# Sorting the first item's values from the loaded layout with strided weight loads, ahead of the key sorts

## Chip, cores, metric

One core of one Trainium2 chip. The metric is the device time of one execution in microseconds (us), read on the chip; lower is better. One execution in each job is also profiled, and all the profile lines below come from such traces.

## The reference, cut to what matters

For each of 4 items and 8 heads, a sort network is normalised to an 8 x 8 matrix P (five rounds of exp and of row and column sums). P mixes the 8 blocks (96 tokens each) of keys and of values; attention runs within a block; a two-layer network with a maximum follows over all 3072 tokens.

```python
for _ in range(5):                       # "the normalising chain"
    P = np.exp(P - max); P /= rowsum; P /= colsum
k_sorted = einsum('bhij,bhjcd->bhicd', P, k_b)     # "key sort"
v_sorted = einsum('bhij,bhjcd->bhicd', P, v_b)     # "value sort": c = 96 tokens, d = 64 columns
attn = softmax(scale * q_b @ k_sorted.T);  x = attn @ v_sorted
out = np.maximum(x @ w1, x @ w2) @ w_out
```

## The kernel before

TensorE multiplies a *stationary* operand, brought in by a weight load (LDWEIGHTS, PEld in the profile), with a *moving* one. A value sort takes v with (head, block) on 64 partitions as stationary operand, 96 tokens of one d at a time, padded to 128 columns; the moving operand is a 64 x 64 block-diagonal matrix of P. Four sorts of 16 matmuls make one item. v arrives as `(c d)` along a partition, so the 96 tokens of one d lie 64 elements apart. The kernel turns it first, with copies, to `(d c)`:

```python
    def turn_v(rows, eng, c0, c1):          # copies on ScalarE ("A") or VectorE ("D")
        dst = v_dc[rows, 0 : D * BLK].rearrange("p (d c) -> p d c", c=BLK)[:, :, c0:c1]
        src = v_raw[rows].rearrange("p (c d) -> p d c", d=D)[:, :, c0:c1]
    ...
    def sort_v(b, t, n=0, eng=None):
        ps = ps_f32("v_ps")                 # PSUM: four buffers in a ring for everything
        keep_streaming(ps, n)               # "fillers": matmuls of zeros, n columns, that keep TensorE busy
        for m in range(16):
            d = t * 16 + m
            nc.tensor.matmul(ps[:, m * 64 : (m + 1) * 64],
                v_dc[r0 : r0 + 64, d * BLK : d * BLK + 128],   # 128 neighbouring columns
                bd_v[b][r0 : r0 + 64, :], start=True, stop=True)
        evac(v_sb[...], ps[...], eng=eng)   # copy out of PSUM on ScalarE or VectorE
    ...                                     # start of the program
    keep_streaming(ps_f32("fill_ps"), 18 * 512)
    for it in range(5):
        sinkhorn(it)                        # from it = 3 on with 6 fillers of 512 columns each
        ...                                 # masks; turn_v in pieces on ScalarE at it = 2, 3
    ...
    sort_k(0, 0, 2048, "A"); sort_k(0, 1, 512, "A"); sort_k(0, 2, 256, "D")
    q_transposes(0, 0, "D")                 # needs q from HBM
    sort_v(0, 0, 256, "A"); ...; sort_v(0, 3, 384, "A")
    q_transposes(0, 1, "D"); scores(0, 0, 256); scores(0, 1, 256); values(0, 0, 512)
```

The softmax here doesn't subtract the row's maximum and nothing guards it: scores larger than these inputs give would overflow.

## Time and profile before

| | before |
|---|---|
| median (range) | 181.52 us (181.5 to 182.01), 3 runs |
| span of the profiled run, granted TensorE clock | 179.5 us, 0.999 |
| TensorE busy | 95% |
| first product of the dense layer (h_ps) starts | 25.93 us |
| TensorE's waits from 16 to 90 us | 0.22, 0.20, 0.35 and 0.60 us |

TensorE is the bound from about 16 us on. "Clock" is the granted clock as a share of full speed.

### The profile page before, as it was taken

How to read it: one execution, taken by the hardware profiler on the slowest of the kernel's cores; microseconds unless marked ns; L12 is line 12 of the kernel's file. 1: busy time of each engine (PE TensorE's matmuls, PEld its weight loads, DVE VectorE, ACT ScalarE, POOL GpSimd, SP SyncE). 2: the span in 40 equal slices, each digit the busy share in tenths (PEclk: the TensorE clock that was granted, in tenths of full speed). 3: DMA queues.
4: the chain of work that ended last, by engine and by line, in shares of the span. 5: the costliest groups of instructions: out<-in, count | busy, mean ns of one | idle time of the engine just before them, and what ended most of it. 6: DMA issues, size and time to landing. Idle time of an engine off the chain costs nothing.

```text
span 179.5 us, 4648 instructions
## 1 busy us (share of the span) xinstructions
PE 170.0 (95%) x2083; PEld 100.7 (56%) x2083; DVE 94.0 (52%) x192; ACT 91.8 (51%) x110; POOL 22.9 (13%) x39
## 2 busy tenths in 40 slices
PE   7797989999999989999989999999999999999993
PEld 2246666666565535577655554657555546554453
DVE  5878498559864395253586436156245415340210
ACT  3695876777664445368784341465833233520021
POOL 7861443200180000001000000000000000000000
PEclk9999999999999999999999999999999999999999
DMA  3999999999299991235600113200001132000333
GB/s 58 201 204 206 200 207 214 194 202 208 55 120 221 206 250 48 99 117 74 108 4 0 57 63 117 104 17 5 0 4 42 74 117 116 4 0 4 117 117 117
DMA packets 13939, 19.17 MB, mean 107 GB/s; under 512 B 800, under 2 KB 8864, under 8 KB 13920
## 3 DMA queue, kind: packets, MB, share of 16 engines
q0 software_dynamic: 10304, 12.58, 41.6%
q1 hardware_dynamic: 3328, 6.10, 8.9%
q8 instruction: 16, 0.26, 0.6%
q10 hardware_dynamic: 288, 0.20, 0.3%
q14 instruction: 3, 0.02, 0.0%
HBM read 25.17 MB, written 6.29 MB: 175 GB/s over the span
## 4 chain that ended last, share of the span: by engine, by line
PE 58%; DMA 29%; DVE 5%; issue 4%; POOL 2%; ACT 1%; POOLq 0%; DVEq 0%
PE out_ps L590 32%; PE h_ps L563 16%; DMA v_raw<-in_v_dram 10%; DMA w_sb<-in_moe_w_dram 10%; DMA q_raw<-in_q_dram 9%; PE o_ps L463 3%; PE tx_ps L495 2%; PE k_ps L371 2%; PE s_ps L438 2%; DVE g L579 2%; PE tq_ps L341 1%; DVE x L480 1%; DVE xT L105 1%; POOL v_raw L153 1%; DVE v_dc L209 1%
## 5 line engine op out<-in xcount | busy, mean ns | idle before, releaser
L590 PE MATMUL out_ps<-wo_sb,g 128*128 128x512 bf16 (+2 forms) x208 | 48.1, 363 | 0.2 <-DVE g L579 0.2
L563 PE MATMUL h_ps<-xT,w_sb 128*128 128x384 bf16 x256 | 46.1, 326 | 0.5 <-DVE g L579 0.2
L563 PEld LDWEIGHTS <-w_sb 128*128 128x128 bf16 x256 | 23.6, 97 | 15.1 <-issue 0.7
L577 ACT ACTIVATE g<-h_ps 128x768 bf16<-128x768 f32 x24 | 19.4, 811 | 23.4 <-PE h_ps L563 23.4
L446 ACT ACTIVATE e<-s_ps 96x768 bf16<-96x768 f32 x32 | 24.1, 804 | 14.0 <-PE s_ps L438 13.9
L590 PEld LDWEIGHTS <-g 128*128 128x128 bf16 x208 | 17.7, 97 | 15.8 <-issue 0.2
L590 PE MATMUL out_ps<-wc,xT 128*128 128x512 bf16 (+2 forms) x104 | 25.0, 362 | 0.0
L103 ACT COPY o<-out_ps 128x1024 f32<-128x1024 f32 x8 | 8.1, 1012 | 31.0 <-PE out_ps L590 27.3
L480 DVE TENSOR_TENSOR x<-o_ps,rs 96x512 bf16<-96x512 f32 x32 | 22.0, 687 | 1.1
L474 DVE RECIPROCAL rs<-o_ps 96x8 f32<-96x8 f32 x32 | 6.4, 201 | 27.4 <-PE o_ps L463 27.2
L590 PEld LDWEIGHTS <-xT 128*128 128x128 bf16 x104 | 9.9, 98 | 10.9
L209 DVE COPY v_dc<-v_raw 64x1536 bf16<-64x1536 bf16 (+2 forms) x9 | 14.1, 1583 | 1.8 <-DMA v_raw<-in_v_dram 1.7
L463 PEld LDWEIGHTS <-e 96*128 96x128 bf16 x256 | 11.2, 98 | 6.5 <-DVE x L480 1.1
L579 DVE TENSOR_SCALAR g<-h_ps 128x768 bf16<-128x768 f32 x8 | 7.7, 958 | 13.5 <-PE h_ps L563 10.6
L463 PE MATMUL o_ps<-v_sb,e 96*128 96x65 bf16 x256 | 12.9, 193 | 1.3 <-DVE x L480 0.6
L105 DVE CAST v_sb<-v_ps 96x1024 bf16<-96x1024 f32 x7 | 8.5, 1217 | 5.9 <-PE v_ps L392 3.9
L103 ACT CAST v_sb<-v_ps 96x1024 bf16<-96x1024 f32 x9 | 8.7, 1010 | 3.4 <-PE v_ps L392 2.6
L103 ACT CAST kT<-k_ps 128x1024 bf16<-128x1024 f32 x10 | 9.5, 1024 | 0.0
L103 ACT COPY xT<-tx_ps 128x768 bf16<-128x768 bf16 x11 | 8.8, 797 | 1.5 <-PE tx_ps L495 1.5
L438 PEld LDWEIGHTS <-kT 64*128 64x128 bf16 x256 | 6.2, 94 | 5.4 <-issue 4.4
L129 POOL DMA_DIRECT2D q_raw<-in_q_dram x4 | 3.6, 901 | 43.0 <-DVE q_pair L326 40.7
L438 PE MATMUL s_ps<-qT,kT 64*128 64x96 bf16 x256 | 9.0, 204 | 0.1
(78 smaller groups left out, 162.5 us busy)
## 6 DMA issues: line engine op xcount, KB each, us to landing
out_dram<-o SPq DMA_DIRECT2D x11, 512.0 KB, 2.8
k_raw<-in_k_dram POOLq DMA_DIRECT2D x12, 256.0 KB, 13.7
q_raw<-in_q_dram POOLq DMA_DIRECT2D x4, 768.0 KB, 8.9
v_raw<-in_v_dram POOLq DMA_DIRECT2D x6, 384.0 KB, 12.0
w_sb<-in_moe_w_dram POOLq DMA_DIRECT2D x3, 512.0 KB, 15.7
wo_sb<-in_moe_w_out_dram POOLq DMA_DIRECT2D x2, 512.0 KB, 19.9
v_raw<-in_v_dram POOLq DMA_DIRECT2D x3, 256.0 KB, 5.1
w_sb<-in_moe_w_dram POOLq DMA_DIRECT2D x2, 256.0 KB, 14.3
```

What stands on the lines that cost most here:

```text
L103: nc.scalar.copy(out=out_ap, in_=in_ap)
L105: nc.vector.tensor_copy(out=out_ap, in_=in_ap)
L209: nc.vector.tensor_copy(out=dst, in_=src)
L438: nc.tensor.matmul(ps[:, h2 * 512 + ii * BLK : h2 * 512 + (ii + 1) * BLK], kT[b][rows, (hp * 8 + i) * BLK : (hp * 8 + i) * BLK + 128], rhs ...
L446: nc.scalar.activation(out=e[:, 0 : 8 * BLK].rearrange("p (t f) -> p t f", t=2), in_=ps[0:BLK].rearrange("p (t f) -> p t f", t=2)[:, :, 0 ...
L463: nc.tensor.matmul(ps[:, h2 * 512 + ii * 65 : h2 * 512 + (ii + 1) * 65], e[:, (h2 * 4 + ii) * BLK : (h2 * 4 + ii) * BLK + 128], v_sb[:, m0 ...
L474: nc.vector.reciprocal(out=rs, in_=ov[:, :, :, 64])
L480: nc.vector.tensor_tensor(out=x, in0=ov[:, :, :, 0:D], in1=rs.to_broadcast([BLK, 2, 4, D]), op=ALU.mult,)
L563: nc.tensor.matmul(h_ps[t][:, m * 512 : m * 512 + TCH], w1_sb[:, hp, fb * 128 : (fb + 1) * 128], xT[:, b % 2, ch, hp % 2, hp // 2, :], sta ...
L577: nc.scalar.activation(out=g, in_=src, func=AF.Relu)
L579: nc.vector.tensor_scalar(out=g, in0=src, scalar1=0.0, scalar2=None, op0=ALU.max)
L590: nc.tensor.matmul(dst, g_tiles[b, ch, m // 2][:, m % 2, off : off + 128] if m < NFB else xT[:, b % 2, ch, hp % 2, hp // 2, off : off + 12 ...
```

## The change

The intent: drop the turn of item 0's v (five copies) and load the weights with a step of 64 elements straight from the loaded layout, so that the value sorts no longer hang on the turn. They can then run ahead of the key sorts, in the time in which TensorE waited for q. Fillers are shortened.

```diff
-    v_raw = big.tile([128, BLK * D], BF16, tag="v_raw", name="v_raw")
+    v_raw = big.tile([128, 128 * D], BF16, tag="v_raw", name="v_raw")
+    nc.vector.memset(v_raw[:, BLK * D :], 0.0)
...
-        kinds = [1] if b % 2 else [1, 0]
+        kinds = [1] if b % 2 else [0, 1]     # the matrix for the values is built first
...
-                v_dc[r0 : r0 + 64, d * BLK : d * BLK + 128],
+                v_raw[0:64].rearrange("p (c d) -> p d c", d=D)[:, d]
+                if b == 0
+                else v_dc[r0 : r0 + 64, d * BLK : d * BLK + 128],
...
-    turn_v(first, "A", ...)                  # all five turns of item 0
-    sort_k(0, 0, 2048, "A")
-    sort_k(0, 1, 512, "A")
-    sort_k(0, 2, 256, "D")
+    sort_v(0, 0, 2048, "A")
+    sort_v(0, 1, 128, "D")
+    sort_k(0, 0, 128, "A")
+    sort_k(0, 1, 128, "D")
+    sort_k(0, 2, 128, "A")
     q_transposes(0, 0, "D")
-    sort_v(0, 0, 256, "A")
-    sort_v(0, 1, 384, "A")
-    sort_v(0, 2, 384, "D")
-    sort_v(0, 3, 384, "A")
+    sort_v(0, 2, 128, "A")
+    scores(0, 0, 256)
+    sort_v(0, 3, 128, "D")
+    scores(0, 1, 256)
     q_transposes(0, 1, "D")
-    scores(0, 0, 256)
-    scores(0, 1, 256)
-    values(0, 0, 512)
+    values(0, 0, 256)
```

More of the change, by code (lines that the diff above doesn't have):

```diff
@@ L204, in turn_v @@
         dst = v_dc[rows, 0 : D * BLK].rearrange("p (d c) -> p d c", c=BLK)[:, :, c0:c1]
-        src = v_raw[rows].rearrange("p (c d) -> p d c", d=D)[:, :, c0:c1]
+        src = v_raw[rows, 0 : BLK * D].rearrange("p (c d) -> p d c", d=D)[:, :, c0:c1]
         if eng == "A":
@@ L647 @@
             selections(0)
-            turn_v(first, "A", 0, 11)
-        if it == 3:
-            turn_v(first, "A", 11, 22)
-    turn_v(first, "A", 22, 40)
     block_diagonals(0)
-    turn_v(first, "D", 56, 96)
-    turn_v(first, "A", 40, 56)
     SC, VA, TR = att(0)
-    sort_k(0, 0, 2048, "A")
-    sort_k(0, 1, 512, "A")
-    sort_k(0, 2, 256, "D")
+    sort_v(0, 0, 2048, "A")
[3 more added lines that the diff above has]
+    sort_k(0, 2, 128, "A")
     q_transposes(0, 0, "D")
-    sort_v(0, 0, 256, "A")
-    sort_v(0, 1, 384, "A")
-    sort_v(0, 2, 384, "D")
-    sort_v(0, 3, 384, "A")
+    sort_v(0, 2, 128, "A")
+    scores(0, 0, 256)
+    sort_v(0, 3, 128, "D")
+    scores(0, 1, 256)
     q_transposes(0, 1, "D")
-    scores(0, 0, 256)
-    scores(0, 1, 256)
-    values(0, 0, 512)
+    values(0, 0, 256)
     SC[2]()
```

## The prediction

> **What bounds the kernel now.** I read three views in this order: the page (busy time and the slices), TensorE's instructions in order of time for the first 45 us, and those of VectorE and ScalarE for the same stretch. The page says that TensorE is the bound:
>
> ```profile
> PE 170.0 (95%) x2083; PEld 100.7 (56%) x2083; DVE 94.0 (52%) x192; ACT 91.8 (51%) x110; POOL 22.9 (13%) x39
> PE   7797989999999989999989999999999999999993
> DMA  3999999999299991235600113200001132000333
> ```
>
> From the sixth slice (4.5 us each) on, TensorE is nearly always full; the only gap over 0.35 us after 16 us is one of 0.60 us at 64.4. So what the change can win lies in the start: whatever moves the first dense products earlier moves the end by as much, unless a load holds them. The start, as TensorE lived it (start, duration, what, and in brackets the idle time before it):
>
> ```profile
> 12.46 0.69 PE L371 MATMUL k_ps<-bd,k_raw 64*64 64x64 bf16 x32
> 15.91 0.86 PE L346 MATMUL tq_ps<-ident,q_raw 128*64 128x128 bf16 x24 [0.97 <-DMA q_raw<-in_q_dram]
> 16.92 0.64 PE L392 MATMUL v_ps<-bd,v_dc 64*128 64x64 bf16 x16
> 19.43 0.64 PE L392 MATMUL v_ps<-bd,v_dc 64*128 64x64 bf16 x16
> 20.00 0.86 PE L346 MATMUL tq_ps<-ident,q_raw 128*64 128x128 bf16 x24
> 22.26 0.42 PE L463 MATMUL o_ps<-v_sb,e 96*128 96x65 bf16 x8
> 22.61 0.51 PE L438 MATMUL s_ps<-qT,kT 64*128 64x96 bf16 x16
> 25.93 0.81 PE L563 MATMUL h_ps<-xT,w_sb 128*128 128x384 bf16 x4
> ```
>
> The reader is to see: the key sorts come first, TensorE then waits 0.97 us for the load of q, and all four value sorts run after that wait, on the path to the scores and the first product. They can't run earlier because the turned copy of v isn't complete until the last of these ends, near 15.3 us (VectorE) and 13.75 us (ScalarE):
>
> ```profile
> 12.91 2.38 DVE L209 COPY v_dc<-v_raw 64x2560 bf16<-64x2560 bf16 x1
> 9.73 4.02 ACT L207 COPY v_dc<-v_raw 64x1152 bf16<-64x1152 bf16 x2
> ```
>
> [...] these rows show the 128-column load shorter than the 64-column one.
>
> ```profile
> L392 PEld LDWEIGHTS <-v_dc 64*128 64x128 bf16 x64 | 2.1, 95 | 0.6 <-issue 0.5
> L346 PEld LDWEIGHTS <-q_raw 128*64 128x64 bf16 x48 | 1.4, 110 | 1.1 <-DMA q_raw<-in_q_dram 1.1
> ```
>
> [...] here the granted clock is 0.999 over the whole span[...].
>
> **The change, part by part.**
>
> *Removed:* five turning copies of item 0. On ScalarE they are 1.39 + 1.38 + 4.02 = about 6.8 us, on VectorE 2.38 us. All lie before 15.3 us. ScalarE's do not delay its exponentials (each starts 0.04 us after the VectorE result it needs), so the copies cost only through the order that they force: value sorts after key sorts, and evacuations queued behind copies.
>
> *Added:* one VectorE memset of 1024 words of 4 bytes. The memset of 256 words took 0.27 us, so about 1.07 us, at 1.4 to 2.5 us or a little later. The first row sum starts at 2.61, so the normalising chain slips by 0 to 0.4 us. Most of that falls into slack ahead of the load of q. I count 0.1.
>
> *Moved:* two value sorts and all key sorts now stand ahead of the q turn; value sorts 2 and 3 stand around the first scores. The order of instructions also shows a gain that the diff doesn't: the static balance of evacuations hands one relu of item 0 from VectorE to ScalarE, and reshuffles six evacuations of item 2 (four of values, one of q, several relus).
>
> *The sum.* From starts in TensorE's timeline: one value sort takes 17.49 - 16.92 = 0.57 us (36 ns a matmul), one key sort 0.63, one half of the q turn 0.79, 8 scores 0.28. A filler of 256 columns costs 0.21 from start to start, of 384 0.27, of 512 0.32; the line through these gives 0.16 for 128. If a strided load costs no more than a contiguous one, TensorE runs: value sort 0 at 12.46 (after the same 2048-column filler), to 13.03; value sort 1 to 13.76; three key sorts at 0.79 each to 16.13. q has landed at 15.9, so the 0.97 us wait is filled with work. Then q turn to 16.92, value sort 2 to 17.65. The first scores need the q evacuation on VectorE (0.96 us from 16.98), so 17.95 to 18.25; value sort 3 to 18.98; scores 1 to 19.47; second q turn to 20.26. VectorE evacuates value sort 3 (1.22 us from 19.0) and then the second q half, to about 21.3; the third and fourth scores (22.61 before) need that half. So they start at about 21.3: **1.3 us earlier.**
>
> Does a weight load eat that? The difference of the first weight tile is done on GpSimd at 22.94, and the first product, at 25.93 - 1.3 = 24.6, stays behind it. The tighter one is the third difference on VectorE, whose weights landed at 27.2 (chain of waits: the load of w from 9.78 for 17.39 us). It started at 27.31; VectorE would now reach it at 26.0 and wait 1.2 us. Behind it on VectorE stand 1.23 us (evacuation of w2T) and 0.68 us (fourth difference), so the next softmax quotient would start at 29.65 and not at 29.3, its result come at 30.5, and the third pair of h products, which takes over its PSUM buffer, could start at 30.5; the full shift asks for 31.83 - 1.3 = 30.53. It just fits. So 1.3 us passes, but a larger gain would not.
>
> Then strided loads: 4 sorts x 16 = 64 loads, all on this path now. Each extra 10 ns costs 0.64 us. At 36 ns a matmul the gain is 1.3; at 56 it is gone.
>
> Later: with one relu less on VectorE (0.96 us), the four turns of item 1 and the two q copies can begin earlier, the loads behind them are issued earlier, and the 0.60 us wait at 64.4 us (VectorE waiting for v, then TensorE for VectorE) should shrink. I count 0.3. Sum with an allowance of 8 ns a load (64 x 8 = 0.5 us): 181.52 - 1.3 - 0.3 + 0.5 + 0.1 = **180.5 us**, 0.6% less.
>
> **The rivals.**
>
> *A: strided loads are free.* [...] so does the change's own tuning (short fillers look measured). Then 179.7 to 180.1. Chance 0.45.
>
> *B: [...]* About 50 to 65 ns a matmul, 64 x 14 to 29 ns = 0.9 to 1.9 us: the gain is cancelled, 180.5 to 181.8. Chance 0.27.
>
> *C: [...] the penalty is several-fold.* [...] Against it: nobody would shift these sorts onto the path without having seen them run. Chance 0.2.
>
> *D: the weights' landing binds.* TensorE arrives earlier and waits, with the gain falling to 0.5: 181. By my sums it just doesn't. It is the wait that would take the place of the one removed: 0.03.
>
> *E: fewer fillers let the clock drop* near 16 to 24 us, costing 1 to 3 us. The gaps I foresee are under 1 us, so I give it little, 0.05.
>
> **Range and chances.** A and B together fill 179.5 to 181.8; half of C reaches to 184. Range 179.3 to 184.0. Faster by over 2% needs under 177.9, a gain of 3.6 us. That is more than all the value sorts' share of the start, and the weights' landing at 27.2 stands against it: 0.03. Slower by over 2% needs over 185.2, so loads at least (185.2 - 180.0)/64 = about 80 ns dearer than contiguous ones: 0.11. The rest, 0.86, is within 2%.
>
> **What would show each step right or wrong.** Right: no turning copies before 16 us; value sort 0 at about 12.5 us, of 0.6 us; no wait for q over 0.3 us; the scores that stood at 22.61 at about 21.3, the first h products at 24.6; VectorE waiting near 26 to 27.2 for weights. A value sort's start to next start of 0.57 says A, 0.8 to 1.0 says B, 1.7 or more says C. D shows as an idle TensorE at 28 to 31 us, E as a clock under 0.99 in the slices. The prediction is wrong if loads of value sorts are over 100 ns apart, [...] or if the reshuffled evacuations of item 2 add waits at 85 to 95 us where VectorE held TensorE for only 0.24 us twice.

## The result, and the profile after

| | before | after |
|---|---|---|
| median (range) | 181.74 us (181.5 to 182.01), 4 runs | 186.69 us (185.72 to 187.79), 4 runs |
| ratio of fast runs | | 1.0277, 95% interval 1.0227 to 1.0326 |
| span, clock of the profiled run | 179.5 us, 0.999 | 185.7 us, 0.963 |
| first h product starts | 25.93 us | 32.00 us |

Ratios here are the mean time of one kernel's fast runs over that of the other's in the same rounds, so not quite the ratio of the medians quoted. All eight runs count as fast (within 1.5% of the fastest of the same kernel). The change makes the kernel 2.8% slower; the range of the prediction ended at 184.0.

The page of the changed kernel; the rows are 40 slices of 4.6 us, in tenths:

```profile
PE 178.3 (96%) x2083; PEld 108.4 (58%) x2083; DVE 92.4 (50%) x191; ACT 85.3 (46%) x107; POOL 23.0 (12%) x39
...
PE   7899999989999999999999999999999999999993
...
PEclk9997855999999999999999999999999999999999
```

TensorE is busier than before and the time is longer: busy time alone cannot tell useful work from slow work. The last row shows what no row before showed: a clock below full speed in four slices. TensorE's order of time (start, duration, what):

```profile
12.70 1.60 PE L393 MATMUL v_ps<-bd,v_raw 64*128 64x64 bf16 x16
14.40 1.60 PE L393 MATMUL v_ps<-bd,v_raw 64*128 64x64 bf16 x16
16.09 0.94 PE L372 MATMUL k_ps<-bd,k_raw 64*64 64x64 bf16 x32
...
19.39 1.01 PE L347 MATMUL tq_ps<-ident,q_raw 128*64 128x128 bf16 x24
...
20.49 1.64 PE L393 MATMUL v_ps<-bd,v_raw 64*128 64x64 bf16 x16
...
22.71 1.63 PE L393 MATMUL v_ps<-bd,v_raw 64*128 64x64 bf16 x16
...
25.03 1.49 PE L347 MATMUL tq_ps<-ident,q_raw 128*64 128x128 bf16 x24
...
27.57 0.83 PE L441 MATMUL s_ps<-qT,kT 64*128 64x96 bf16 x16 [0.29 <-DVE qT L105]
...
32.00 1.49 PE L566 MATMUL h_ps<-xT,w_sb 128*128 128x384 bf16 x4
```

A value sort takes 14.23 - 12.70 = 1.53 us from its start to the next start, where it took 0.57. Over its 16 matmuls that is 96 ns each, where it was 36, start-up included. (From matmul to matmul inside a contiguous sort it is 29 ns, inside a strided one about 90.) The wait for q is gone, as meant: the q turn starts at 19.39 with no idle time before it. But it starts 3.5 us later than before. Then ordinary work is slow too: the second q turn takes 1.49 us, the first 1.01, and both took 0.86 before; four h products take 1.49 us in place of 0.81. The table of stretches says why (columns: stretch and its length; busy time of each engine with its instructions; the clock; DMA share; GB/s):

```profile
core 0: us, PE busy (x) PEld busy (x) DVE busy (x) ACT busy (x) POOL busy (x), PEclk, DMA share, GB/s
14.00:16.00 2.00, 2.00 (x22) 1.85 (x21) 0.00 (x0) 1.01 (x1) 0.00 (x0) 1.00 1.26 203
16.00:18.00 2.00, 2.00 (x65) 1.75 (x66) 1.22 (x1) 0.93 (x1) 0.54 (x1) 0.58 1.28 202
...
20.00:22.00 2.00, 2.00 (x33) 1.84 (x27) 0.96 (x1) 0.51 (x1) 2.00 (x2) 1.00 1.27 201
...
24.00:26.00 2.00, 2.00 (x33) 1.57 (x34) 1.22 (x1) 0.81 (x1) 0.53 (x1) 0.50 1.27 213
26.00:28.00 2.00, 1.71 (x31) 1.41 (x29) 1.40 (x3) 0.00 (x0) 0.41 (x1) 0.50 1.22 200
```

At 14 to 16 us, with a full clock, the strided loads are already slow; the loads are therefore not slow because of the clock. By the clock records of the trace it falls twice: at 16.32 us (back at 19.74), just after the first two strided sorts, and at 23.15 (back at 33.39), within the fourth. From the first h product to the end the two kernels take the same time: 185.7 - 32.0 = 153.7 us against 179.5 - 25.9 = 153.6. So the net loss lies in the start. (The two totals hide a small exchange: the changed kernel runs the first 1.4 us of that part at half clock, about 0.7 us lost by estimate, and saves about as much later, as e10 will show.)

### The profile page after: what moved, and what is told of

Read it like the earlier page. It is cut to its first block, busy times and chain, and to the rows that moved or that the text cites. A ratio compares the mean times of both kernels' runs of the same rounds, so it can differ in the third digit from the quotient of the medians.

```text
span 185.7 us, 4642 instructions
## 1 busy us (share of the span) xinstructions
PE 178.3 (96%) x2083; PEld 108.4 (58%) x2083; DVE 92.4 (50%) x191; ACT 85.3 (46%) x107; POOL 23.0 (12%) x39
## 4 chain that ended last, share of the span: by engine, by line
PE 73%; DVE 12%; DMA 7%; ACT 3%; issue 1%; POOL 1%; DVEq 0%; ACTq 0%
PE out_ps L593 31%; PE h_ps L566 21%; DMA v_raw<-in_v_dram 6%; PE o_ps L466 3%; PE v_ps L393 3%; PE k_ps L372 3%; DVE v_dc L210 3%; PE tx_ps L498 3%; PE s_ps L441 3%; ACT g L580 3%; DVE x L483 2%; PE tq_ps L342 1%; PE tq_ps L347 1%; DVE xT L105 1%; PE tw_ps L521 1%
## 5 line engine op out<-in xcount | busy, mean ns | idle before, releaser
L566 PE MATMUL h_ps<-xT,w_sb 128*128 128x384 bf16 x256 | 46.8, 329 | 0.4 <-ACT g L580 0.2
L580 ACT ACTIVATE g<-h_ps 128x768 bf16<-128x768 f32 x28 | 22.6, 812 | 24.8 <-PE h_ps L566 24.8
L105 DVE CAST v_sb<-v_ps 96x1024 bf16<-96x1024 f32 x9 | 10.9, 1219 | 12.1 <-PE v_ps L393 9.0
L466 PEld LDWEIGHTS <-e 96*128 96x128 bf16 x256 | 12.1, 102 | 5.9 <-DVE x L483 0.6
L466 PE MATMUL o_ps<-v_sb,e 96*128 96x65 bf16 x256 | 13.8, 200 | 0.7 <-ACT e L449 0.4
L210 DVE COPY v_dc<-v_raw 64x1536 bf16<-64x1536 bf16 (+1 forms) x8 | 11.8, 1489 | 1.3 <-DMA v_raw<-in_v_dram 1.2
L105 DVE COPY qT<-tq_ps 128x1536 bf16<-128x1536 bf16 x8 | 7.5, 953 | 5.6 <-PE tq_ps L342 3.7
L441 PEld LDWEIGHTS <-kT 64*128 64x128 bf16 x256 | 6.7, 98 | 5.9 <-issue 4.6
L441 PE MATMUL s_ps<-qT,kT 64*128 64x96 bf16 x256 | 9.6, 213 | 0.4 <-DVE qT L105 0.3
L103 ACT CAST v_sb<-v_ps 96x1024 bf16<-96x1024 f32 x7 | 6.9, 1009 | 5.9 <-PE v_ps L393 5.9
```

The source lines that it names most:

```text
L103: nc.scalar.copy(out=out_ap, in_=in_ap)
L105: nc.vector.tensor_copy(out=out_ap, in_=in_ap)
L210: nc.vector.tensor_copy(out=dst, in_=src)
L441: nc.tensor.matmul(ps[:, h2 * 512 + ii * BLK : h2 * 512 + (ii + 1) * BLK], kT[b][rows, (hp * 8 + i) * BLK : (hp * 8 + i) * BLK + 128], rhs ...
L466: nc.tensor.matmul(ps[:, h2 * 512 + ii * 65 : h2 * 512 + (ii + 1) * 65], e[:, (h2 * 4 + ii) * BLK : (h2 * 4 + ii) * BLK + 128], v_sb[:, m0 ...
L566: nc.tensor.matmul(h_ps[t][:, m * 512 : m * 512 + TCH], w1_sb[:, hp, fb * 128 : (fb + 1) * 128], xT[:, b % 2, ch, hp % 2, hp // 2, :], sta ...
```

## Experiments

Theory: (1) a load of 128 columns 64 elements apart costs some 60 ns more than one of neighbours, 64 times 60 = 3.8 us; (2) in a strided sort TensorE streams 64 columns in 96 ns and waits for weights for most of it, and this low share of streaming lets the clock fall; (3) the new order by itself gains. Rivals: the shortened fillers let the clock fall; or the new order itself loses.

To compare runs I use a measure worked out from the traces, the *streaming share*: moving columns of all matmuls that start within a stretch of 3.4 us, divided by 2.4 columns a ns and the length of the stretch (a share can come out over 1, because starts are counted). The rate is that of the traces, rounded up: six products of 512 columns take 1.30 us at full clock, 2.36 columns a ns. The 3.4 us are the shortest stretch at half clock: between 10 and 70 us each such stretch in these traces lasts 3.41 us or two, three or four times that (3.41 and 10.24 in the changed kernel, 6.83 in e1, 13.65 in e2). That the clock follows the share over just this length is my assumption.

### e1_contig: the change with contiguous loads (wrong result)

```diff
-                v_raw[0:64].rearrange("p (c d) -> p d c", d=D)[:, d]
+                v_raw[0:64, d * BLK : d * BLK + 128]
```

> The changed kernel with one thing undone: the value sorts of item 0 load 128 neighbouring columns of the raw v in place of columns 64 elements apart (so the result is wrong, on purpose). Same order, fillers, memset, waits. My theory (the strided loads cost 96 ns a matmul in place of 36, and their low share of streaming lets TensorE's clock drop): value sort 0.57 us, clock 0.99 or more, 180.2 us, 1 to 1.6 us under the kernel before. Rival F (the shortened fillers let the clock drop, not the loads): clock stays near 0.965 and the time is 182.5 to 184. Rival G (the new order itself loses): slower than before with a full clock.

Measured: 181.74 us (180.57 to 182.79), ratio 1.0013 (0.9967 to 1.0059). The value sort is back at 0.57 us. But the gain of the order isn't there, and the clock of the four runs was 0.981, 1.0, 1.0 and 0.991. Loads explain most of the 5 us, but both my theory (180.2, full clock) and the rivals miss. The trace shows something that nobody had named:

```profile
18.70 0.29 PE L393 MATMUL v_ps<-bd,v_raw 64*128 64x64 bf16 x4
20.20 0.52 PE L393 MATMUL v_ps<-bd,v_raw 64*128 64x64 bf16 x12 [1.21 <-issue]
```

TensorE stops for 1.2 us in the middle of a value sort, between two matmuls that need nothing from anybody ("issue": no releaser in the profile). e6 and e10 take this up.

### e2_wide: the change with a wider moving operand

```diff
-                ps[:, m * 64 : (m + 1) * 64],
+                ps[:, m * 64 : m * 64 + wide],     # wide = min(192, what is left of the 512 columns)
...
-                bd_v[b][r0 : r0 + 64, :],
+                bd_wide...[0:64, 0:wide]           # bd_v, then 128 columns of zeros
```

> The changed kernel with the strided loads kept, but each matmul of item 0's value sorts streams up to 192 columns in place of 64 (the rest are zeros, overwritten by the next matmul; the result stays right). [...] My theory: sort stays at 1.53 to 1.6 us, clock goes back to 0.99 or more, about 184.0 us: the clock's share, 2.5 to 3 us, is won back, the loads' share of 3.8 us isn't. If the clock does not hang on the share of streaming: no change from 186.7.

Measured: 185.14 us (183.93 to 188.51), correct; ratio of the three fast runs 1.0174. By execution: 183.93 and 184.11 us with a clock of 1.0, 185.14 with 0.991, 187.03 with 0.972, 188.51 with 0.962. The sort stays at 1.58 us, where 64 columns took 1.53 to 1.57, so the extra columns are nearly free under the loads (192 columns are 81 ns by estimate, at the measured 2.36 a ns, and a strided sort takes 96 ns a matmul). With a full clock the time is the 184.0 that I expected. But the clock was full in only two of five executions. The traced one (0.962) again has a stall with no releaser, 0.39 us at 22.46, and the clock falls just there. e13 finishes this.

### e3_old_order: the kernel before with strided loads only

```diff
 (kernel before; turns, order and fillers kept, memset of the tail added)
-                v_dc[r0 : r0 + 64, d * BLK : d * BLK + 128],
+                v_raw[0:64].rearrange("p (c d) -> p d c", d=D)[:, d]   # for b == 0
```

> The kernel before with one thing added: its four value sorts of item 0 load strided from the raw v (with the memset of the tail), while the turning copies are still done and order and fillers are those of before. My theory: loads 64 x 60 ns = 3.8 us and a drop of the clock worth 2 to 3 us in spite of the long fillers: 187 to 188.5, clock about 0.96. Rival F (short fillers are the cause of the clock): clock stays at 0.99 or more, 185.5.

Measured: 187.37 us (186.89 to 188.13), ratio 1.0329, correct; clock 0.972 to 0.982 in all four runs. The strided loads alone (with the memset), in the old order with the old, longer fillers, lose at least as much as the whole change: the intervals, 1.0299 to 1.0359 and 1.0227 to 1.0326, overlap. So the short fillers are not needed for the clock to fall, and the order is not what loses.

```profile
17.11 1.62 PE L393 MATMUL v_ps<-bd,v_raw 64*128 64x64 bf16 x16
...
22.91 1.63 PE L393 MATMUL v_ps<-bd,v_raw 64*128 64x64 bf16 x16
24.48 1.49 PE L347 MATMUL tq_ps<-ident,q_raw 128*64 128x128 bf16 x24
```

The sorts take the same 1.6 us at full clock (1.62 at 17.11) and at half (1.63 at 22.91), where the q turn needs 1.49 us in place of 0.86. So these strided sorts take the same time at either clock.

### e4_sweep_a and e5_sweep_b: the step

```diff
-                v_raw[0:64].rearrange("p (c d) -> p d c", d=D)[:, d]
+                v_raw[0:64, m : m + 127 * step + 1 : step]     # another step for every eight loads (e5: v_raw and its memset longer)
```

> The changed kernel with the 64 loads of the value sorts at column steps of 1, 2, 4, 8, 16, 32, 64 and 63 elements, eight loads each (wrong result, on purpose). Read is the time from one matmul's start to the next. [...] 36 ns at steps 1, 2 and 4, about 96 from 8 on, 63 like 64. [...] If it is a clash of powers of two: growing from 8 to 64, and 63 fast again.

> As the first sweep, with column steps of 48, 56, 60, 62, 65, 66, 72 and 96 elements (wrong result, on purpose; a longer memset delays the start, so only the distance between matmuls is read). The first sweep gave 29 ns at steps 1 and 2, 33 at 4, 60 to 62 at 8, 16, 32 and 63, and 96 at 64. If 64 is slow because its step is a multiple of 128 bytes: all eight here at about 60. If because large steps are slow and 63 is an exception: 65, 66, 72 and 96 at 90 or more.

Measured, from one matmul's start to the next in the trace, the first of each eight left out:

| step, elements of 2 bytes | 1 | 2 | 4 | 8 | 16 | 32 | 48 to 63 | **64** | 65, 66, 72, 96 |
|---|---|---|---|---|---|---|---|---|---|
| ns a matmul | 29 | 29 | 32 to 35 | 59 to 61 | 60 to 64 | 57 to 65 | 58 to 68 | **87 to 98** | 57 to 67 |

(One 800 ns gap, at step 64, and one 975 ns gap, at 72, are left out as the stall of e1; so are the intervals that followed them, 113 and 29 ns. Step 64 is left with four intervals, but the 64 loads of the changed kernel show the same.) Up to step 4 the stride is nearly free: 29 to 35 ns. From step 8 on the load takes twice the time, 57 to 68 ns, whatever the step, but for one. Why the cost comes between 4 and 8 is not shown. The step of 64, that is 128 bytes, is worse than all others that I tried: about 90 ns, where 63 and 65 take about 60. Why is not shown, and no other multiple of 64 was tried; it is not the size of the step and not its power of two as such (8, 16 and 32 are ordinary). The change had hit the one bad step of the sixteen tried.

### e6_fetch: what the stall is

```diff
-            w = min(n, 512)
+            w = min(n, 512 if by is None else 256)   # the twelve late fillers become twenty-four; on e1_contig
```

> The run with contiguous loads again (wrong result, on purpose), with the twelve late fillers of 512 columns split into twenty-four of 256: the same columns, twelve matmuls more ahead of all real work. [...] Then the stall without a releaser stays at matmul 223 by count, so it moves twelve matmuls earlier in the work (from inside value sort 3 to the end of value sort 2 or the first scores)[...]. If the stall hangs on the place in the work (a buffer, a wait that the profile does not show), it stays inside value sort 3, now matmul 235.

Measured: 184.01 us (a single run, so its state is unknown; clock 0.972). The stall moved to another place in the work, into the first scores:

```profile
18.27 0.20 PE L441 MATMUL s_ps<-qT,kT 64*128 64x96 bf16 x1
19.66 0.35 PE L441 MATMUL s_ps<-qT,kT 64*128 64x96 bf16 x7 [1.19 <-issue]
```

By count it stayed where it was: TensorE stops ahead of its matmul number 223 (from 0; in e2 and e5 it is 222), in e1 in value sort 3, here in the scores, as 12 more matmuls stand before. So it hangs on the count and not on the place in the work. The profile has a DMA queue of the kind "instruction", 16 packets of 16,384 bytes. In the traces of before and after, the first of them starts when 175 and 180 weight loads have begun, the last when 1995 have, in both: one packet to 121 pairs of weight load and matmul, on average. I read the packets as the program on its way to TensorE, and the stall as a wait for it (the "fetch" of the expectations). That is a guess from the count and the times, as the profile names no releaser. I compared the first packet of that queue (columns below give start and end) and pair 223 in the traces (us; a pair starts with its weight load):

| kernel | packet | last weight load ahead of the stall | pair 223 |
|---|---|---|---|
| before | 17.35 to 18.32 | none | 19.79 |
| after | 19.79 to 20.73 | none | 23.03 |
| e1 | 17.74 to 18.71 | 18.77 | 20.19 |
| e2 | 20.21 to 21.15 | 21.82 | 22.46 |
| e4 | 17.95 to 18.89 | 19.59 | 20.45 |
| e5 | 22.36 to 23.30 | 23.73 | 24.70 |
| e6 | 17.29 to 18.22 | 18.09 | 19.65 |
| e7 | 17.16 to 18.25 | none | 20.07 |

Where there was a stall, the last weight load ahead of it started between 0.13 us before the end of the packet and 0.70 us after it, and pair 223 starts 1.3 to 1.6 us after that end; where there was none, 1.5 to 2.3 us after it. In none of these traces does pair 223 start sooner than 1.3 us after the packet has ended. The kernel that gets there faster waits. The kernel before just doesn't (1.47 us after the packet); the changed one is slowed by its loads and doesn't either (2.30 us); e1 is faster and waits. So, by this reading, the gain of the order in e1 was turned into a wait for the program. When exactly a packet is asked for isn't shown.

### e10_contig_blocks: e1 with matmul 223 earlier in the work (wrong result)

```diff
 (e1_contig)
-    keep_streaming(ps_f32("fill_ps"), 18 * 512)
+    keep_streaming(ps_f32("fill_ps"), 89 * 104, None, 104)   # 89 matmuls of 104 columns: about as many columns, 71 matmuls more
```

> The run with contiguous loads (wrong result, on purpose) with its first eighteen fillers of 512 columns cut into eighty-nine of 104: about the same columns, 71 matmuls more before 7.2 us[...]. Theory of the fetch: no stall inside value sort 3, TensorE streams on, clock at 0.99 or more, 180.2 to 180.8 us, so the order's gain that the prediction counted (1.3 us) comes through. If the stall was not a fetch: the stall near 19 us stays and the time is near 181.7.

The start-up fillers run when TensorE has nothing else to do. With 71 more of them matmul 223 falls 71 matmuls earlier in the work. Measured: 179.61 us (179.45 to 179.91), ratio 0.9888 (0.9867 to 0.9909), clock 0.998 to 1.0 in all four runs. TensorE's order of time has no stall left:

```profile
18.77 0.64 PE L393 MATMUL v_ps<-bd,v_raw 64*128 64x64 bf16 x16
...
25.04 0.81 PE L566 MATMUL h_ps<-xT,w_sb 128*128 128x384 bf16 x4
```

The short fillers and the new order, then, cost no clock: the rivals of the theory fall. The order's gain, in which the dropped turns and the shorter fillers are counted too, is 181.63 - 179.61 = 2.0 us, and the h products start 0.9 us earlier. The rest comes later: from that start to the end it is 152.8 us, against 153.6 before; the wait of 0.60 us at 64.4 us is gone. Against e1 the gain is 2.1 us, more than the stall of 1.2 us. The traced e1 also ran 6.8 us at half clock, but an execution of e1 with a full clock still took 181.66 us, so part of that difference stays open. VectorE waits for the landing of w, TensorE doesn't:

```profile
27.14 0.69 DVE L191 TENSOR_TENSOR w_sb<-w_sb 128x1024 bf16<-128x1024 bf16 x1 [0.65 <-DMA w_sb<-in_moe_w_dram]
```

### e12_before_blocks: the control for e10

```diff
 (kernel before)
-    keep_streaming(ps_f32("fill_ps"), 18 * 512)
+    keep_streaming(ps_f32("fill_ps"), 89 * 104, None, 104)
```

> Control: the kernel before with its first eighteen fillers cut into eighty-nine of 104 columns, nothing else. Its matmul 223 ran at 19.8 us[...], so it was not held up visibly: no change, 181.2 to 181.8 us. If it gained 1% by itself, the contiguous run's gain with blocks would not be the order's.

Measured: 183.43 us (181.99 to 185.6), correct; ratio of the fast runs 1.0069 (1.004 to 1.0098). I missed: it does not stay the same, it loses. The traced run was one of the two slow ones (185.35, clock 0.981). In it q lands later, so that TensorE's wait for q grew from 0.97 to 1.72 us:

```profile
16.64 0.86 PE L346 MATMUL tq_ps<-ident,q_raw 128*64 128x128 bf16 x24 [1.72 <-DMA q_raw<-in_q_dram]
```

The first packet of the instruction queue now lies at 9.59 to 10.57 us (17.35 to 18.32 before), amid the loads of the inputs. It may be what delays q; I did not test that. For e10 the control says enough: cutting the fillers brings nothing by itself, so e10's gain needs the order. But cutting them isn't free here either (a ratio of 1.0069), so e10 and e13, which both cut them, are best compared with each other.

### e13_wide_blocks: strided loads with a high streaming share and the start-up fillers cut

```diff
 (e2_wide)
-    keep_streaming(ps_f32("fill_ps"), 18 * 512)
+    keep_streaming(ps_f32("fill_ps"), 89 * 104, None, 104)
```

> The changed kernel with strided loads, the wide matmuls (up to 192 columns) and the first fillers cut into eighty-nine: right result. The wide matmuls alone gave full clock in two of five executions (184.0 us there) and a lower clock in three; its trace showed a stall at matmul 223 in value sort 3 just ahead of the drop. If a low share of streaming is what lowers the clock, with both causes of a low share gone the clock is 0.995 or more in at least four of six executions and the time 183.4 to 184.4 us; what is left over before, about 2.3 us, is the loads' price less the order's gain (3.8 less 1.5). If strided loads themselves lower the clock, it stays at 0.96 to 0.98 in most.

Measured: 183.36 us, correct; five runs from 183.33 to 183.45 with a clock of 0.998 to 1.0, and one slow run (186.49, clock 0.972). Ratio of the fast runs 1.0095 (1.0081 to 1.0109). The strided sorts are as long as in the changed kernel, within 0.05 us, but each load now goes with 192 moving columns, not 64, and the clock stays:

```profile
14.46 1.64 PE L399 MATMUL v_ps<-bd,v_raw 64*128 64x192 bf16 x16
```

Against e10 only the loads and the zeros that stream under them differ: 183.36 - 179.61 = 3.75 us. The four sorts are 4.0 us longer in the traces (6.30 against 2.28), and the first h product starts 3.8 us later. Against the changed kernel, 186.7 - 183.4 = 3.3 us, what the half clock cost, with whatever the cut fillers do by themselves. That median lies between two groups: 185.7 and 185.9 us at a clock of 0.972, 187.5 and 187.8 at 0.963, which lose 2.5 and 4.3 us against e13. No run cuts the start-up fillers and keeps strided loads of 64 columns. That the cut alone brings the clock back is unlikely, as the changed kernel has no stall at matmul 223 and e2, with the fillers uncut, had two executions with a full clock; but this is argued and was not run.

The streaming share in the 3.41 us that end where the clock falls, in every traced run in which it fell:

| | e5 | e4 | e9 | after | e11 | after, second | e3 | e6 | e2 | e12 | e8 | e1 |
|---|---|---|---|---|---|---|---|---|---|---|---|---|
| the clock falls at (us) | 10.56 | 21.09 | 20.49 | 16.32 | 66.98 | 23.15 | 18.91 | 19.86 | 22.36 | 17.90 | 19.12 | 22.08 |
| share before | 0.25 | 0.35 | 0.36 | 0.37 | 0.38 | 0.57 | 0.58 | 0.58 | 0.59 | 0.60 | 0.66 | 0.66 |

Only what lies before the fall may be counted, since a half clock lowers the share itself (four h products take 1.49 us there, 0.81 at full clock). For comparison I cut the 14 traces with a clock record into steps of 3.41 us, in phase with the clock's changes, from 8.5 us on. That gives 637 steps at full clock. The clock fell after 5 of 5 with a share below 0.5, after 7 of 19 between 0.5 and 0.67, and after none of 613 above. So in these traces a low share goes with the fall, and the 0.37 of the changed kernel is below every step that left the clock full (0.54 and up). What decides between 0.5 and 0.67, where the falls of e1, e2, e3 and the second one of the changed kernel lie, is not shown. In the changed kernel no gap of TensorE in the slow stretches was over 0.3 us, and none at all lies in the 3.4 us before the first fall. It ran 3.41 + 10.24 = 13.7 us at half clock, as the mean clock says too: 2 x (1 - 0.963) x 185.7.

### e7, e8, e9, e11: the order with a turn that costs less

Can the order's gain be had with a right result? The sort by d lets the turn be cut by d: ScalarE turns the first half ahead of the sorts, VectorE the second after the masks. Value sorts 0 and 1 then go ahead of key sorts 1 and 2; value sorts 2 and 3 stay around the first scores. Loads stay contiguous.

```diff
 (e7, from the kernel before)
-    turn_v(first, "A", ...)                       # pieces cut by token; one of the five on VectorE
+    turn_v(first, "A", 0, 22, 0, 32); turn_v(first, "A", 22, 44, 0, 32); turn_v(first, "A", 44, 96, 0, 32)
+    turn_v(first, "D", 0, 96, 32, 64)             # tokens 0..95, d = 32..63
 (e8)  32 becomes 33
 (e9)  e8, with the start-up fillers in 89 pieces of 104 columns
 (e11) e9, with 34
```

> A version meant to be right and no slower than the kernel before: loads stay contiguous, the turning copies are cut by column (d 0 to 31 on ScalarE ahead of the sorts, d 32 to 63 on VectorE beside them), so that value sorts 0 and 1 run ahead of the wait for q, with fillers of 256 columns. Without the fetch limit: 180.4 us (1.1 us off). [...] TensorE stalls near 20 us for about 1 us and the gain shrinks to 0.3 us or nothing: 181.0 to 181.6. Clock 0.99 or more in most executions, since no loads are strided.

> The half turn with its flaw mended: the last load of value sort 1 reads 128 columns, 32 of them of d = 32, so it waited 1.05 us for VectorE's half; ScalarE now turns d 0 to 32. Theory of the fetch: that wait goes, but a stall without a releaser appears at matmul 223[...], and nothing is won: 181.3 to 182.5. Without a fetch limit: 180.6.

> The mended half turn with the first fillers cut into eighty-nine of 104 columns, as in the contiguous run: right result, contiguous loads, no stall[...] if the theory of the fetch holds. Then 180.5 to 181.0 us, 0.4 to 0.6% under the kernel before, with the clock at 0.99 or more. Without: like the mended half turn alone.

> The half turn with blocks again, cut at d = 34 in place of 33. Cut at 33, VectorE's copy of 2976 elements a row took 5.3 us; cut at 32, 3072 took 2.8 us. If an odd start[...] halves VectorE's rate, the copy from 34 takes about 2.6 us, the wait of 1.8 us for VectorE before value sort 2 goes, the clock holds, and the version comes to the contiguous run's time or a little above: 179.6 to 180.6 us, 0.6 to 1.1% under the kernel before, with a right result. If the slow copy has another cause: 184 to 185 again.

| | e7, cut at 32 | e8, cut at 33 | e9, 33, fillers cut | e11, 34, fillers cut |
|---|---|---|---|---|
| median (range) | 182.85 (181.66 to 183.78) | 185.22 (183.93 to 185.39) | 185.2 (184.92 to 185.71) | 180.39 (180.04 to 184.66) |
| ratio of fast runs | 1.0068 | 1.0181 | 1.0195 | 0.9925 |

All four are correct, and all but e11 miss what was expected of them. e7 has a slip of mine: the last load of value sort 1 reads 128 columns, of which 32 belong to d = 32, so it waits 1.05 us for VectorE's copy. e8 should have mended that, and got worse, because VectorE's copy took nearly twice as long; e9, with the start-up fillers cut, waits for the same copy (TensorE stands idle for 1.83 us ahead of value sort 2). VectorE's order of time in e7, e8 and e11:

```profile
12.92 2.79 DVE L209 COPY v_dc<-v_raw 64x3072 bf16<-64x3072 bf16 x1
```

```profile
13.14 5.29 DVE L209 COPY v_dc<-v_raw 64x2976 bf16<-64x2976 bf16 x1
```

```profile
13.14 2.65 DVE L209 COPY v_dc<-v_raw 64x2880 bf16<-64x2880 bf16 x1
```

In e8 it copies fewer elements than in e7 (31 d, not 32), but takes 1.78 ns an element in place of 0.91. TensorE then stood idle for 2.18 us ahead of value sort 2, and the clock fell. Cutting at 34 (e11) takes the cost away: 2.65 us, 0.92 ns an element. I had forecast this from the odd start of the source, which was a guess, but the cut at 33 also makes the number of d odd (31, against 32 and 30). These runs change both at once, so which of the two costs the time is not shown.

e11 gives a right result and beats both kernels, by 0.75% over the kernel before (interval of the ratio 0.991 to 0.994), in four of six executions, 180.04 to 180.46 us. The other two took 183.07 us with a full clock and 184.66 us; in the latter, which is the traced one, VectorE waited 3.85 us at 63.5 us for a load of item 2's v, and TensorE 2.68 us for VectorE. Whether that is a rare delay of a transfer or belongs to this order is open; with the two slow ones the mean of e11 is 181.5 us, no gain worth the name over 181.6.

## Why the prediction was wrong

The step that failed is the cost of a strided load. The sum carried "an allowance of 8 ns a load (64 x 8 = 0.5 us)" and put 0.72 of the chance on A (free loads) and B. Measured are 60 ns more a load and 3.75 us (e13 against e10). That is between B and C of the rivals, nearer C; a sort took 1.53 us, where 0.8 to 1.0 was to say B and 1.7 or more C. B gave 50 to 65 ns a matmul, an estimate, as no costly weight load in the trace of before is strided. That about holds for 63 and 65 elements (57 to 68 ns at every other step from 8 up, e4 and e5), but not for the 64 of this kernel (87 to 98). Why 64 is special stays open.

The second failed step is E, "the gaps I foresee are under 1 us, so I give it little". There were hardly any gaps, and the clock fell in every execution, at a cost of about 3.3 us. I looked for idle time, where the runs point to the share of streaming (0.37 and 0.57 ahead of the two falls). And I took E for a rival of C, when here the slow loads brought E about: a matmul that waits 96 ns for its weights streams, by estimate, for 27 of them (64 columns at the measured 2.36 a ns). For the same reason the bound "loads at least (185.2 - 180.0)/64 = about 80 ns dearer" for a loss of 2% was too high: 60 ns and the clock were enough. The argument against C, that nobody would shift these sorts without having seen them run, was no evidence.

The other steps:

- The order's gain was predicted as 1.3 us at the start and 0.3 later, less 0.1 for the memset. Freed of the rest (e10) it is 0.9 and 0.8 in the traced runs, and 2.0 us between the medians. Right in mechanism, somewhat small in size; the split between start and later was off. What I did not know of is the stall at matmul 223, 1.2 us in e1, which took the gain away there; in the changed kernel it is no loss, because that kernel gets to this matmul only at 23.03 us, 2.30 us after the packet, and has no stall.
- The memset: 0.1 us predicted, about 0.2 measured (the first matmul of the masks starts at 11.58 us, 11.35 before, and the first sort at 12.70, 12.46 before).
- The wait for q is gone, as predicted. D was right too: VectorE waits for w at 27.1 us in e10, and TensorE doesn't.
- The evacuations of item 2 cost nothing: VectorE held TensorE at 85 to 95 us for 0.24 us twice before; after, ScalarE held it once for 0.19.
- The load itself: by shape, the row of the changed kernel (11 to 26 us) that answers to the one of before, 95 ns a load, is this, 210 ns:

```profile
L393 PEld LDWEIGHTS <-v_raw 64*128 64x128 bf16 x64 | 6.0, 210 | 0.6 <-issue 0.4
```
- That "the granted clock is 0.999 over the whole span" reads too much into the figure: the clock records of that trace begin at 5.22 us. Before that, fillers of 512 columns start 0.43 us apart, and 0.22 after it, so the first 5 us ran at half clock.

The sum, all from medians of fast runs: 181.65 (before) - 2.0 (order, e10) + 3.75 (loads, e13 - e10) + 3.3 (clock, after - e13) = 186.7, and 186.69 was measured. It closes by construction, since its terms are differences from one run to the next; that the loads' term comes to four times the 0.96 us by which a sort grew (3.84), and that e13's clock is full, are what support it.

## What to carry to other kernels

A copy that was saved by reading an operand in place came back here in each weight load: 57 to 68 ns a matmul at steps of 8 elements (16 bytes) and more, and 87 to 98 at 64 elements, in place of 29. Time one such load before reordering around it, and try a pitch other than 128 bytes. Where weight loads outlast the matmuls they serve, ask for the share of time in which TensorE streams, not for idle gaps, before trusting the clock: here it fell after 5 of 5 steps with a share below 0.5, and in the changed kernel with no gap in the 3.4 us before the first fall. And when a stretch of many small matmuls gets faster, look for waits without a releaser at a fixed count of matmuls (222 or 223 here, up to 1.2 us), and after cutting a 16-bit VectorE copy at an odd element, look at its time (5.29 us cut at 33, where 32 and 34 took 2.79 and 2.65).
